# Attention with a tanh softcap, then soft mixture-of-experts slots: transposes, logits and slot sums at fixed steps of a two-quad period

## The chip, the core and the metric

The kernel runs on one core of one Trainium2 chip. Its engines work side by side, each with its own instruction queue: TensorE (PE) for matmuls and transposes into PSUM, VectorE (DVE), ScalarE (ACT), GpSimd (POOL), and SyncE (SP), which here only issues transfers. GpSimd issues transfers as well. The metric is the device time in microseconds (us) from start to end of one execution.

## What is computed

Eight batches of twelve heads, 448 positions, head size 64, float32 inputs; then a soft mixture of experts over all 3584 positions with 32 slots.

```python
scores = (q @ k.T) / sqrt(64)                 # per batch and head: 448 x 448
scores = cap * tanh(scores / cap)             # cap = 30
attn = exp(scores - max); attn /= attn.sum()  # over keys
x = concat_heads(attn @ v)                    # 3584 x 768

logits = x @ phi                              # 3584 x 32
d = exp(logits - max over positions); d /= d.sum(over positions)
slot_input = d.T @ x                          # 32 slots x 768, four slots per expert
slot_out[e] = relu(slot_input[e] @ w1[e]) @ w2[e]        # 8 experts, 768 -> 1024 -> 768
c = softmax(logits over slots)
out = c @ slot_out                            # 3584 x 768
```

The maxima are not subtracted in the kernel: tanh bounds the scores by 30, and the logits are small.

## The kernel before

**Quads, pairs, tiles, chunks.** A *quad* `Q` is four heads of one batch; three quads make a batch, 24 quads the whole. `load(Q)` fetches q, k and v of a quad with three transfers on SP (L119), each into a float32 tile of which there is one buffer, so a new load waits until the old content has been cast. `cast` (L126, VectorE) makes bfloat16 of q or k; `transp` (L134) transposes it on TensorE in seven 128x128 pieces and copies the result from PSUM (L136, VectorE) to `qT` or `kT`, two buffers each. `vcast` (L144, L145, GpSimd) puts v into one of two block-diagonal tiles `vbd` with a column of ones, which yields the row sums.

A quad is two *pairs* of heads (48 pairs). A pair has `NT` = 7 *tiles* of keys, numbered c = 0 to 6. Four tiles, wherever a pair begins or ends, make a *chunk* (`CH` = 4; 84 chunks). The chunk is the unit of ScalarE's work: one tanh (L170) over four PSUM banks of scores `sc`, one exp (L173) in place on the bfloat16 result `ex`. `sc` has one buffer of four banks: the scores of chunk j+1 (`qk_chunk`, L164, eight matmuls) can start only when the tanh of chunk j has read it, so they are made while ScalarE does the exp of chunk j.

`pv_tile` (L185) multiplies one tile of `ex` with `vbd`: four matmuls into two PSUM banks, `pv0` and `pv1`, one buffer each. A pair accumulates over its seven tiles. After the last (c = 6) VectorE takes the reciprocal of the row sums and scales, once for each bank (L194, L195), into `xq`. The next pair's first matmul into a bank waits until that bank has been read.

**Behind a pair.** `x_transp` (L207, L209) transposes the pair's part of `xq` with four transposes and a copy. `logits` (L217, L222) multiplies a quad's two transposed pairs with phi in eight matmuls and adds to the batch's sum. After a batch's third quad `e_exp` (L225) takes the exponential on ScalarE, and `slot_sums` (L237) accumulates d.T @ x and the sum of d in 28 matmuls, in three parts, with an addition to the running sum (L244) at the end. All these PSUM results, and those of `transp`, share one pool `psT` of two banks; a slot sum holds one of the two from its first part to its last.

**The order.** The order of each engine's instructions is written out by hand: the program issues each engine's instructions in the order of the Python calls, and waits between engines follow from the data. Small jobs are put by `at(j, ...)` into a list of chunk j. The main loop (L293) issues for each chunk j:

```python
tanh_chunk(j)
pv_tile of the four tiles of chunk j-1
the jobs of list j
qk_chunk(j + 1)
exp_chunk(j)
```

Before, a job's chunk follows from its own quad or pair: casts four chunks ahead of the quad's first, and so on (L257 to L276). The transfers of the expert weights w1 and w2 (32 of them, L280) are spread over the chunks on GpSimd's queue; the remaining eight blocks of w2 (L317) follow when the memory of the attention stage becomes free.

**The tail.** After the last chunk the remaining jobs run, then the expert matmuls (L337, L388), the combine weights (`ET4`, L367) and the output (L401 to L408).

Of the kernel before, what the change touches and what calls it, by code (L numbers as in the profile page):

```python
# [16 lines left out]
NT = 7  # L17
DH = 64
S = 448
CH = 4  # L20
# [7 lines left out]
def kernel(  # L28
# [22 lines left out]
    NQB = H // 4  # L51
    NQ = B * NQB
    NPAIR = 2 * NQ
    NTILE = NPAIR * NT
    NCH = NTILE // CH
# [99 lines left out]
    def qk_chunk(j):  # L155
        sc = psS.tile([P, CH, 512], F32, name="sc", tag="sc")
        scores[j] = sc
        for u in range(CH):
            pr, c = divmod(j * CH + u, NT)
            Q, h = divmod(pr, 2)  # L160
            r = slice(h * HP, h * HP + HP)
            for i in range(2):
                cs = slice(i * HP, i * HP + HP)
                pe.matmul(sc[cs, u, 0:S], qkT["k", Q][r, c, cs],  # L164
                          qkT["q", Q][r, :, cs], start=True, stop=True)

    def tanh_chunk(j):
        ex = exps.tile([P, CH, S], BF16, name="ex", tag="ex")
        exs[j] = ex
        act.activation(ex, scores.pop(j)[:, :, 0:S], ACT.Tanh, scale=qk_scale / cap)  # L170

    def exp_chunk(j):
        act.activation(exs[j], exs[j], ACT.Exp, scale=cap)  # L173

    def pv_tile(t):
        j, u = divmod(t, CH)
        pr, c = divmod(t, NT)
        Q, h = divmod(pr, 2)
        if c == 0:
            pvs[pr] = [psV.tile([P, 2, VW], F32, name=f"pv{s}", tag=f"pv{s}")  # L180
                       for s in range(2)]
            if h == 0:
                xq[Q] = xs.tile([P, NG, 2 * P], BF16, name="xq", tag="xq")
        for g in range(NG):
            pe.matmul(pvs[pr][g // 2][:, g % 2, :],  # L185
                      exs[j][:, u, GOFF[g]:GOFF[g] + P],
                      vbds[Q % 2][:, h, c, :],
                      start=(c == 0 and g % 2 == 0), stop=(c == NT - 1),
                      skip_group_check=True)
        if c == NT - 1:  # L190
            for s in range(2):
                pv = pvs[pr][s].rearrange("p g (i w) -> p g i w", i=2)
                rec = xs.tile([P, 2, 2, 1], F32, name="rec", tag="rec", bufs=4)
                dve.reciprocal(rec, pv[:, :, :, DH:DH + 1])  # L194
                dve.tensor_tensor(  # L195
                    xq[Q][:, 2 * s:2 * s + 2, h * P:(h + 1) * P]
                    .rearrange("p g (i d) -> p g i d", i=2),
                    pv[:, :, :, 0:DH],
                    rec.to_broadcast([P, 2, 2, DH]), op=ALU.mult)
            pvs.pop(pr)  # L200
# [48 lines left out]
    aux = {}  # L249

    def at(j, f, *a):
        aux.setdefault(max(j, 0), []).append((f, a))

    def first_chunk(Q):
        return Q * 2 * NT // CH

    for Q in range(1, NQ):  # L257
        j0 = first_chunk(Q)
        at(j0 - 4, cast, "k", Q)
        at(j0 - 4, cast, "q", Q)  # L260
        at(j0 - 3, transp, "k", Q)
        at(j0 - 3, vcast, Q)
        if Q + 1 < NQ:
            at(j0 - 3, load, Q + 1)
        at(j0 - 2, transp, "q", Q)
    for pr in range(NPAIR):
        jc = (pr * NT + NT - 1) // CH + 1
        Q, h = divmod(pr, 2)
        b, hq = divmod(Q, NQB)
        at(jc + 1, x_transp, pr)  # L270
        if h == 1:
            at(jc + 2, logits, Q)
            if hq == NQB - 1:
                at(jc + 3, e_exp, b)
                for part in range(3):
                    at(jc + 4 + part, slot_sums, b, part, 3)  # L276
    nw = len(wjobs)
    for n, job in enumerate(wjobs):
        j = 2 + n * (NCH - 8) // nw
# [12 lines left out]
    qk_chunk(0)  # L292
    for j in range(NCH):  # L293
        tanh_chunk(j)
        if j > 0:
            for t in range((j - 1) * CH, j * CH):
                pv_tile(t)
        for f, a in aux.pop(j, []):
            f(*a)
        if j + 1 < NCH:  # L300
            qk_chunk(j + 1)
        exp_chunk(j)
    for t in range((NCH - 1) * CH, NCH * CH):
        pv_tile(t)
# [10 lines left out]
    for n0 in range(R2, len(blocks), 4):  # L315
        t = tl.tile([P, 4, D], BF16, name=f"w2t{n0}")
# [129 lines left out]
```

The softmax here doesn't subtract the row's maximum and nothing guards it: scores larger than these inputs give would overflow.

## Time and profile before

| | us |
|---|---|
| median of three runs | 377.85 (368.37, 377.85, 377.98) |
| profiled execution, its own time | 366.62 |
| its span, first to last instruction | 364.5 |
| first tanh starts | 10.88 |
| last exp ends, about | 299.7 |

Busy time in three stretches of the profiled execution, from the profile's table of stretches (us; in brackets the number of instructions):

| stretch | PE | DVE | ACT | POOL | granted PE clock | DMA engines busy |
|---|---|---|---|---|---|---|
| 0 to 10.88 | 3.56 (22) | 3.92 (4) | 1.28 (1) | 8.63 (20) | 1.00 | 0.79 |
| 10.88 to 299.70 | 211.35 (2878) | 130.72 (356) | 277.19 (175) | 66.46 (80) | 0.98 | 0.74 |
| 299.70 to 364.50 | 41.51 (416) | 23.91 (43) | 16.62 (22) | 4.46 (6) | 0.69 | 0.85 |

The middle stretch is the attention stage, 289 of 364.5 us. The granted clock is a share of TensorE's full speed; it comes from the records of the trace. Transfers that are issued there take, from issue to landing, in the median: q 3.5 us, k 4.3, v 3.6 (448 KB each), w1 6.6 (512 KB), w2 8.2 (768 KB).

A profile names for each idle stretch of an engine what ended it (the releaser). The "chain of work that ended last" goes back from the last instruction of the execution, at each step to what released it, or to the instruction ahead of it on its engine.

### The profile page before, as it was taken

Reading aid. Unit: us, or ns where it says so; the run is one execution under the profiler, and the core shown is the slowest. Engines: PE = TensorE matmul, PEld = TensorE weight load, DVE = VectorE, ACT = ScalarE, POOL = GpSimd, SP = SyncE. Lnnn points to the kernel's source line nnn. Section 1 sums busy time; section 2 is a strip of 40 time slices with the busy share of each in tenths; the row PEclk is TensorE's granted clock in tenths of the full one; section 3 lists DMA queues with packets and bytes.
Section 4 is the critical chain, followed back from the end, with each engine's and each line's share of the span. In section 5 each row is a group of like instructions: output and inputs, shape, how many; then the busy total and the mean of one; then the engine's idle time right before and its main releaser. Section 6 shows DMA issues by size and latency. Waiting matters only on the chain.

```text
span 364.5 us, 7663 instructions
## 1 busy us (share of the span) xinstructions
PE 256.4 (70%) x3316; PEld 171.0 (47%) x3316; DVE 158.5 (43%) x403; ACT 295.1 (81%) x198; POOL 79.5 (22%) x106
## 2 busy tenths in 40 slices
PE   2868787767687767686867777778667666687581
PEld 1546455545455545464645545555545443354120
DVE  4244535435444454444553545445435324224452
ACT  1798979999999999999999999999999980214341
POOL 8321231023113230232032302321223004000000
PEclk9998969999999999999999999999999995969755
DMA  8768749476858668667696697899994808993997
GB/s 217 241 160 173 202 140 225 115 199 179 201 114 227 172 177 192 187 187 183 156 217 176 155 245 173 206 228 218 202 237 65 151 2 137 210 175 122 396 398 294
DMA packets 39409, 69.75 MB, mean 191 GB/s; under 512 B 3024, under 2 KB 29648, under 8 KB 39376
## 3 DMA queue, kind: packets, MB, share of 16 engines
q0 software_dynamic: 15760, 25.22, 38.6%
q1 hardware_dynamic: 23616, 44.05, 36.8%
q8 instruction: 26, 0.43, 0.4%
q14 instruction: 7, 0.06, 0.0%
HBM read 83.46 MB, written 11.01 MB: 259 GB/s over the span
## 4 chain that ended last, share of the span: by engine, by line
ACT 51%; PE 23%; DVE 11%; DMA 9%; issue 2%; SPq 0%; DVEq 0%; POOL 0%
ACT ex L173 26%; ACT ex L170 25%; PE pv L185 9%; PE sc L164 7%; DVE xq L195 5%; DMA w2t<-in_moe_w_dram 5%; DMA out_dram<-ob 3%; DVE ob L405 2%; PE so_ps L388 2%; DVE rec L194 2%; PE kps L134 2%; DMA kraw<-in_k_dram 1%; PE op L401 1%; PE qps L134 1%; DVE qT L136 1%
## 5 line engine op out<-in xcount | busy, mean ns | idle before, releaser
L185 PE MATMUL pv<-vbd,ex 128*128 128x130 bf16 x1344 | 107.0, 225 | 69.0 <-ACT ex L173 36.5
L170 ACT ACTIVATE ex<-sc 128x1792 bf16<-128x1792 f32 x84 | 138.9, 1654 | 18.0 <-PE sc L164 17.9
L173 ACT ACTIVATE ex<-ex 128x1792 bf16<-128x1792 bf16 x84 | 142.5, 1696 | 2.4
L185 PEld LDWEIGHTS <-ex 128*128 128x128 bf16 x1344 | 79.8, 100 | 116.1 <-ACT ex L173 71.2
L164 PE MATMUL sc<-qT,kT 64*64 64x448 bf16 x672 | 73.3, 369 | 4.6 <-ACT ex L170 1.9
L144 POOL CAST vbd<-vraw 64x896 bf16<-64x896 f32 x24 | 22.3, 928 | 203.2 <-PE pv L185 199.6
L194 DVE RECIPROCAL rec<-pv 128x4 f32<-128x4 f32 x96 | 17.1, 178 | 71.7 <-PE pv L185 71.7
L195 DVE TENSOR_TENSOR xq<-pv,rec 128x256 bf16<-128x256 f32 x96 | 40.8, 425 | 3.3
L164 PEld LDWEIGHTS <-kT 64*64 64x64 bf16 x672 | 29.1, 107 | 20.3 <-issue 3.3
L136 DVE COPY qT<-qps 128x896 bf16<-128x896 bf16 x24 | 15.0, 624 | 45.0 <-PE qps L134 45.0
L209 DVE COPY xT<-xps 128x512 bf16<-128x512 bf16 x48 | 20.1, 418 | 14.2 <-PE xps L207 14.2
L407 ACT ACTIVATE ob<-op,winv 128x768 f32<-128x768 f32 x14 | 12.5, 901 | 13.6 <-DMA out_dram<-ob 7.2
L401 PE MATMUL op<-so,ET 128*128 128x384 bf16 x56 | 18.1, 425 | 7.6 <-DVE ob L405 4.8
L145 POOL CAST vbd<-vraw 64x896 bf16<-64x896 f32 x24 | 23.0, 957 | 1.4
L207 PE MATMUL xps<-ident,xq 128*128 128x128 bf16 x192 | 19.3, 223 | 3.9 <-DVE qT L136 3.7
L136 DVE COPY kT<-kps 128x896 bf16<-128x896 bf16 x24 | 14.9, 620 | 12.7 <-PE kps L134 12.7
L405 DVE TENSOR_SCALAR ob<-op,winv 128x768 f32<-128x768 f32 x14 | 14.1, 1017 | 11.6 <-DMA out_dram<-ob 6.4
L134 PE MATMUL qps<-ident,qbf 128*128 128x128 bf16 x168 | 14.2, 228 | 5.1 <-DVE qbf L126 5.1
L126 DVE CAST kbf<-kraw 128x896 bf16<-128x896 f32 x24 | 16.0, 667 | 2.7 <-DMA kraw<-in_k_dram 2.7
L280 POOL DMA_DIRECT2D w1b<-in_moe_w_dram x24 | 17.0, 709 | 0.0
L126 DVE CAST qbf<-qraw 128x896 bf16<-128x896 f32 x24 | 15.2, 634 | 4.0 <-DMA qraw<-in_q_dram 4.0
L134 PE MATMUL kps<-ident,kbf 128*128 128x128 bf16 x168 | 14.5, 231 | 2.5 <-DVE kbf L126 2.5
(56 smaller groups left out, 152.4 us busy)
## 6 DMA issues: line engine op xcount, KB each, us to landing
w1b<-in_moe_w_dram POOLq DMA_DIRECT2D x24, 512.0 KB, 6.6
qraw<-in_q_dram SPq DMA_DIRECT2D x24, 448.0 KB, 3.5
kraw<-in_k_dram SPq DMA_DIRECT2D x24, 448.0 KB, 4.3
vraw<-in_v_dram SPq DMA_DIRECT2D x24, 448.0 KB, 3.6
out_dram<-ob SPq DMA_DIRECT2D x28, 384.0 KB, 4.5
w2b<-in_moe_w_dram POOLq DMA_DIRECT2D x8, 768.0 KB, 8.2
w2t<-in_moe_w_dram POOLq DMA_DIRECT2D x8, 768.0 KB, 12.1
phib<-in_moe_phi_dram POOLq DMA_DIRECT2D x1, 48.0 KB, 5.5
```

The source lines that it names most:

```text
L126: dve.tensor_copy(t.rearrange("p c (h d) -> p h c d", h=2), raws.pop((nm, Q)).rearrange("p h (c d) -> p h c d", d=DH))
L134: pe.transpose(ps[:, c, :], src[:, c, :], ident)
L136: dve.tensor_copy(t, ps)
L144: pool.tensor_copy(t[0:HP, :, :, 0:DH], raw[0:HP])
L145: pool.tensor_copy(t[HP:P, :, :, DH + 1:VW - 1], raw[HP:P])
L164: pe.matmul(sc[cs, u, 0:S], qkT["k", Q][r, c, cs], qkT["q", Q][r, :, cs], start=True, stop=True)
L170: act.activation(ex, scores.pop(j)[:, :, 0:S], ACT.Tanh, scale=qk_scale / cap)
L173: act.activation(exs[j], exs[j], ACT.Exp, scale=cap)
L185: pe.matmul(pvs[pr][g // 2][:, g % 2, :], exs[j][:, u, GOFF[g]:GOFF[g] + P], vbds[Q % 2][:, h, c, :], start=(c == 0 and g % 2 == 0), stop= ...
L194: dve.reciprocal(rec, pv[:, :, :, DH:DH + 1])
L195: dve.tensor_tensor(xq[Q][:, 2 * s:2 * s + 2, h * P:(h + 1) * P] .rearrange("p g (i d) -> p g i d", i=2), pv[:, :, :, 0:DH], rec.to_broadc ...
L401: pe.matmul(op[:, half, 0:HD], ET4[:, bb, c, :, :].rearrange("p a q -> p (a q)"), so[:, half, :], start=True, stop=True)
```

## The change

The lists of jobs are filled by a period of `PER` = 7 chunks, which are 28 tiles, four pairs, two quads. With m the number of the period and "step" the chunk number mod 7, a job stands at:

| step | tiles whose PV is issued in it | before, between PV and scores | after |
|---|---|---|---|
| 0 | c = 3 4 5 6 | kT transposes of an odd quad, vcast, x transpose | logits, kT transposes, vcast, q cast |
| 1 | 0 1 2 3 | qT transposes, x transpose (and a slot part) | qT transposes, x transpose |
| 2 | 4 5 6, 0 | logits (and a slot part) | x transpose (and a slot part) |
| 3 | 1 2 3 4 | k and q casts, x transpose (and a slot part) | logits, x transpose, k cast (and a slot part) |
| 4 | 5 6, 0 1 | kT transposes of an even quad, vcast (and a slot part) | kT transposes, vcast, q cast |
| 5 | 2 3 4 5 | qT transposes, x transpose (and a slot part) | qT transposes (and a slot part) |
| 6 | 6, 0 1 2 | k and q casts, logits (and a slot part) | x transpose, k cast (and a slot part) |

A comma in the second column is the turn from one pair to the next inside a chunk. Slot sums come once per batch, every ten or eleven chunks, now in two parts instead of three. The x transpose of a pair comes one chunk later for three of every four pairs; logits and `e_exp` follow one chunk later; each q cast stands one chunk behind its k cast. The weight transfers keep their chunks.

The main loop changes as well. In a chunk with a turn (steps 2, 4, 6), all jobs are issued after the old pair's last matmuls and ahead of the new pair's first. In a chunk without one, the first half of the jobs (rounded up) goes between PV and scores, as before, and the rest behind the scores. At the end, the last pairs' jobs are drawn forward where possible: chunk 83 gets x transposes of pairs 45 and 46 and the logits of quad 22.

```diff
-    for Q in range(1, NQ):
-        j0 = first_chunk(Q)
-        at(j0 - 4, cast, "k", Q)
-        at(j0 - 4, cast, "q", Q)
-        at(j0 - 3, transp, "k", Q)
-        at(j0 - 3, vcast, Q)
-        if Q + 1 < NQ:
-            at(j0 - 3, load, Q + 1)
-        at(j0 - 2, transp, "q", Q)
-    for pr in range(NPAIR):
-        jc = (pr * NT + NT - 1) // CH + 1
-        Q, h = divmod(pr, 2)
+    PER = 2 * 2 * NT // CH
+
+    def quad_in(Q, jk, jq):
+        if 0 < Q < NQ:
+            at(jk - 1, cast, "k", Q)
+            at(jk, transp, "k", Q)
+            at(jk, vcast, Q)
+            at(jq - 1, cast, "q", Q)
+            at(jq, transp, "q", Q)
+            if Q + 1 < NQ:
+                at(jq, load, Q + 1)
+
+    def pair_out(pr, j):
+        if 0 <= pr < NPAIR:
+            at(j, x_transp, pr)
+
+    def quad_out(Q, j):
+        if not 0 <= Q < NQ:
+            return
+        at(j, logits, Q)
         b, hq = divmod(Q, NQB)
-        at(jc + 1, x_transp, pr)
-        if h == 1:
-            at(jc + 2, logits, Q)
-            if hq == NQB - 1:
-                at(jc + 3, e_exp, b)
-                for part in range(3):
-                    at(jc + 4 + part, slot_sums, b, part, 3)
+        if hq == NQB - 1:
+            at(j + 1, e_exp, b)
+            at(j + 2, slot_sums, b, 0, 2)
+            at(j + 3, slot_sums, b, 1, 2)
+
+    for m in range(NCH // PER + 1):
+        j0 = m * PER
+        late = m == NCH // PER
+        quad_in(2 * m + 1, j0, j0 + 1)
+        pair_out(4 * m - 2, j0 - 1 if late else j0 + 1)
+        pair_out(4 * m - 1, j0 + 2)
+        quad_out(2 * m - 1, j0 + 3)
+        pair_out(4 * m, j0 + 3)
+        quad_in(2 * m + 2, j0 + 4, j0 + 5)
+        pair_out(4 * m + 1, j0 + 6)
+        quad_out(2 * m, j0 + 6 if m == NCH // PER - 1 else j0 + 7)
...
         tanh_chunk(j)
-        if j > 0:
-            for t in range((j - 1) * CH, j * CH):
-                pv_tile(t)
-        for f, a in aux.pop(j, []):
+        ready = list(range((j - 1) * CH, j * CH)) if j else []
+        turn = next((n for n, t in enumerate(ready) if n and t % NT == 0), len(ready))
+        for t in ready[:turn]:
+            pv_tile(t)
+        jobs = aux.pop(j, [])
+        first = len(jobs) if turn < len(ready) else (len(jobs) + 1) // 2
+        for f, a in jobs[:first]:
             f(*a)
+        for t in ready[turn:]:
+            pv_tile(t)
         if j + 1 < NCH:
             qk_chunk(j + 1)
+        for f, a in jobs[first:]:
+            f(*a)
         exp_chunk(j)
```

More of the change, by code (lines that the diff above doesn't have):

```diff
@@ L252, in at @@
         aux.setdefault(max(j, 0), []).append((f, a))
-    def first_chunk(Q):
-        return Q * 2 * NT // CH
-    for Q in range(1, NQ):
-        j0 = first_chunk(Q)
-        at(j0 - 4, cast, "k", Q)
-        at(j0 - 4, cast, "q", Q)
-        at(j0 - 3, transp, "k", Q)
-        at(j0 - 3, vcast, Q)
-        if Q + 1 < NQ:
-            at(j0 - 3, load, Q + 1)
-        at(j0 - 2, transp, "q", Q)
-    for pr in range(NPAIR):
-        jc = (pr * NT + NT - 1) // CH + 1
-        Q, h = divmod(pr, 2)
-        b, hq = divmod(Q, NQB)
-        at(jc + 1, x_transp, pr)
-        if h == 1:
-            at(jc + 2, logits, Q)
-            if hq == NQB - 1:
-                at(jc + 3, e_exp, b)
-                for part in range(3):
-                    at(jc + 4 + part, slot_sums, b, part, 3)
+    PER = 2 * 2 * NT // CH
[15 more added lines that the diff above has]
+        at(j, logits, Q)
+        b, hq = divmod(Q, NQB)
+        if hq == NQB - 1:
[13 more added lines that the diff above has]
+        quad_out(2 * m, j0 + 6 if m == NCH // PER - 1 else j0 + 7)
     nw = len(wjobs)
```

## The prediction

> **What bounds the kernel now.** I read the page's list of the costliest groups first, then the waits, then ScalarE's row of the timeline, then the chain of work that ended last. The groups (columns: line, engine, operation, output and input, count | busy us, mean ns of one | idle time before them, and what ended it):
>
> ```profile
> L185 PE MATMUL pv<-vbd,ex 128*128 128x130 bf16 x1344 | 107.0, 225 | 69.0 <-ACT ex L173 36.5
> L170 ACT ACTIVATE ex<-sc 128x1792 bf16<-128x1792 f32 x84 | 138.9, 1654 | 18.0 <-PE sc L164 17.9
> L173 ACT ACTIVATE ex<-ex 128x1792 bf16<-128x1792 bf16 x84 | 142.5, 1696 | 2.4
> ```
>
> ScalarE works 281 us on 84 tanh and 84 exp, and waits 17.9 us for scores. Of these, 8.9 us are the wait for the first chunk. So the attention stage is bound by ScalarE, and all that a change of TensorE's order can win is the time by which scores come late. The first tanh starts at 10.88, the last at 296.32: 285.44 us for 83 chunks. A chunk that waits for nothing takes 3.28 us from tanh to tanh (289.76, 293.04, 296.32 in the timeline), so 83 x 3.28 = 272.2 and the **excess is 13.2 us**.
>
> I call chunk number mod 7 its step: 7 chunks are 4 pairs, so the pattern repeats. Differences of tanh starts, summed by step over the 12 periods, give the excess as: step 0 0.4, step 1 1.9, step 2 0.6, step 3 0.2, **step 4 5.8**, step 5 0.6, **step 6 3.7**. Steps 4 and 6 are those in which the last matmuls of one pair and the first of the next stand in one chunk with few of the old pair ahead. In undisturbed periods step 4 takes 3.59 and step 6 3.57, with slot sums 3.79 both. The chain shows why (start, us, what):
>
> ```profile
> 153.25 0.30 PE pv L185 x2
> 153.56 0.02 issue
> 153.58 0.20 DVE rec L194
> 153.77 0.02 issue
> 153.79 0.42 DVE xq L195
> 154.22 0.10 DVE rec L194
> 154.32 0.02 issue
> 154.34 0.44 DVE xq L195
> 154.78 0.05 issue
> 154.83 0.74 PE pv L185 x10
> 155.57 0.19 PE lps L217 x8
> 155.76 0.89 PE sc L164 x8
> ```
>
> The reader sees a step 6: TensorE ends the pair, stands idle while VectorE empties both PSUM banks (1.2 us), then does the next pair's matmuls, then eight matmuls of logits, and only then the scores. The idle stretch and the logits lie one behind the other. The waits say the same in sum:
>
> ```profile
> PE pv L185 <- DVE xq L195: 23.5, 60, 0.6
> ACT ex L170 <- PE sc L164: 17.9, 28, 8.9
> ```
>
> [...]there is a half-clock spell (mean clock 0.84 in 35 to 57 us; 16 PV matmuls took 1.92 us there at 45.74, 1.08 elsewhere). [...]at 137.64 a weight load of L207 runs 0.70 us before its matmul, which waits. [...]here both pv tiles have one buffer, and the 23.5 us above are the price.
>
> **The change, part by part.** No matmul, copy, activation or transfer is added or removed; all are moved.
>
> *Key transposes in step 4.* Seven transposes (0.48 us from the first, 148.52, to the scores, 149.00) went between PV and scores. Now they stand after the old pair's 8 matmuls, ahead of the new pair's, in the 1.2 us in which TensorE waits for VectorE. Step 4 was 3.59; the chain without them gives 3.11, under 3.28, so excess 0. Nine plain or slot periods win 0.31 or 0.50 each, slot matmuls leaving this step too (0.20). The two in the cold clock: chunk 4 (4.17) loses 0.55 and keeps 0.34; chunk 11 (4.83; scores at 52.63, last PV behind them at 51.64) loses 0.99 and keeps 0.56. Step 4: 5.8 to 0.9.
>
> *Step 6.* Logits (0.28 from 155.41 to 155.69 by the timeline) go to step 0, where no pair turns. In their place one x transpose of 4 (0.27 by weight loads) and, every second period, 16 slot matmuls (8 take 0.31, so 0.62) stand in the idle stretch: from 153.48 (PV weights end) to 154.28, 0.80 us. 0.27 is hidden; 0.89 overhangs by 0.09, but the second bank is free only at 154.83, which leaves room. Scores then start at 155.41, tanh 0.99 later at 156.40: 3.30 against 3.28. I keep 0.05 each, as the price of a tanh that still just waits. Step 6: 3.7 to 0.55. If cover fails, the 0.27 to 0.89 come back one to one.
>
> *Step 1.* Six chunks lose 0.36: a third tile wanted one of two transpose banks while the slot sums held the other, so x transposes waited for the copy of qT (0.52 idle at 137.66 to 138.34 before L207). Now slot sums are not in step 1, and its x transpose goes behind the scores. There it delays only the next PV: scores from 1.67 to 2.61 after tanh, four transposes to 2.9, next PV not before 3.42. The start-up chunk (0.45, transposes at half clock) stays. Step 1: 1.9 to 0.45.
>
> *Steps 0, 2, 3, 5.* Logits, x transposes and slot sums move into steps with room: PV 0.9, slot 0.62, logits 0.28 end 1.95 after tanh, scores may start at 2.37. The 0.5 of chunk 9 falls to about 0.1 (half clock). The small exponential (L225) stays on ScalarE, 0.05 in each of 7 places. These four: 1.8 to 0.8.
>
> *Casts and loads.* POOL's and SP's orders are unchanged. Each q cast goes one step later, behind the evacuation and the kT copy on VectorE, and frees the raw buffer for the next q load; k is queued behind q on SP. In step 4 that cast now ends 3.2 us after tanh (148.11 end of xq, kT copy 0.62, cast 0.62, less 146.22), so k is issued at 149.8 of the old clock instead of 144.15, and beside v and a weight load of POOL. The next k cast is due in step 6, 5.1 us later. k lands in 4.3 us in the median, 6.5 at most. VectorE may stand there until 157.4 before the transposes make scores late (step 0 at 156.06; scores by +2.47, less 0.48 for transposes and 0.62 for the cast). That is **7.6 us from issue to landing**. I cost it at 0. A k cast moved alone costs nothing: its data came long before.
>
> *Tail.* Chunk 83 gains two x transposes and logits, ends PV 3.36 after tanh, and the last PV start at 3.43: 0. The old x transpose after the last PV stood in VectorE's shadow: 0. The 64.8 us behind the last exp are untouched.
>
> **Sum.** Left of 13.2: 0.9 + 0.55 + 0.45 + 0.8 = 2.7, so the gain is 10.5 us. Profiled execution: 366.62 (span 364.5 and 2.1 around it) to 356.1. The runs shown are 368.37, 377.85 and 377.98. The profiled one stands 11.2 below their median and 1.75 below the lowest, which I take as the same mode: 368.37 - 10.5 = **358**. From the median it would be 367.3; the trace cannot show what the 10 us between the runs are, so this is the range's upper part.
>
> **Rivals.** *Half of it stays.* The turns still end late: VectorE, with xT and casts queued behind the evacuation, or TensorE's own pace lets tanh wait 0.15 in all 23 turns of steps 4 and 6 (3.5 us), and the cold spells cost what they did (1.9). Gain 5.1: 361.5 profiled, 363.3 against the lowest run: within 2%. For it: step 6 comes out at 3.30 with no room. Against: step 4 has 0.17.
>
> *Keys come late.* The q, k and v loads now queue together with a 512 or 768 KB weight load. [...]If k takes more than 7.6 us, VectorE stands at the cast with the next reciprocal behind it, and TensorE at the transposes: at 10 us, 2.4 us in each of 11 periods, 26 less 10.5 = 16 slower, 382 to 384. It decides from 8.6 us on, where it eats the gain. Against it: 6.5 is the longest k seen, and v beside a weight load takes 3.6.
>
> *It does not do what it says*, since a transpose in the gap could wait for the evacuation it should cover. By the code x transposes in a gap read a pair that ended two or more chunks before; only chunk 83 reads the fresh one. Then about 366 to 368.
>
> **How the numbers follow.** Forecast 0.72, half stays 0.16, late keys 0.08, no effect 0.04. A change of 2% (7.3 us) is about what a measurement of this kernel can tell from none. Faster by more: 0.72; within, with the half and no effect: 0.20; slower: 0.08. The gain lies between 5 and 13.2: 353 to 363 from the two lower bases, and up to 368 if the timed runs are of the kind of the median. Range 353 to 368.
>
> **What would show it.** Steps 4 and 6 at 3.28 to 3.35; tanh's wait for scores 10 to 11 us, 8.9 of them the first; waits of PV for xq well under 23.5; span about 354; ScalarE's share of the chain from 51% to 70% or more. Wrong: a wait of the k cast for its DMA beyond the start, or steps 4 and 6 still at 3.5.

## The result, and the profile after

| | before | changed |
|---|---|---|
| median of the runs shown, us | 373.11 (367.37 to 377.98, 4 runs) | 384.53 (380.92 to 387.94, 4 runs) |
| profiled execution, us | 366.62 | 384.37 |
| its span | 364.5 | 382.3 |
| attention stage, first tanh to last exp, about | 288.8 | 305.9 |
| TensorE's granted clock in that stage | 0.98 | 0.89 |

The changed kernel is slower: the ratio of its times to those before is 1.041 (95% interval 1.031 to 1.051). The prediction said 358 and is wrong; of its rivals, the one with the late keys named the mechanism and the time (382 to 384). Runs of one kernel differ by up to 7%, so each ratio leaves out those more than 1.5% above their kernel's fastest; the profiled execution of the kernel before is one of its fastest, and those of before_q_late, q_two_buffers, spread and warm_before are among their kernel's slower ones.

From the page of the kernel before, the shares of its chain of work by engine ("issue" is time in which the engine waited for nothing that the profile shows; a name with q is the engine's instruction queue), its group of k casts (columns as in the prediction) and its k transfers (number, size, median us from issue to landing):

```profile
ACT 51%; PE 23%; DVE 11%; DMA 9%; issue 2%; SPq 0%; DVEq 0%; POOL 0%
...
L126 DVE CAST kbf<-kraw 128x896 bf16<-128x896 f32 x24 | 16.0, 667 | 2.7 <-DMA kraw<-in_k_dram 2.7
...
kraw<-in_k_dram SPq DMA_DIRECT2D x24, 448.0 KB, 4.3
```

The same of the changed kernel, with some groups more:

```profile
DMA 35%; PE 20%; ACT 20%; DVE 13%; issue 7%; SPq 2%; POOL 1%; DVEq 0%; ACTq 0%; POOLq 0%
...
L170 ACT ACTIVATE ex<-sc 128x1792 bf16<-128x1792 f32 x84 | 138.9, 1653 | 35.4 <-PE sc L164 35.2
...
L126 DVE CAST kbf<-kraw 128x896 bf16<-128x896 f32 x24 | 15.3, 639 | 42.0 <-DMA kraw<-in_k_dram 42.0
...
L134 PE MATMUL kps<-ident,kbf 128*128 128x128 bf16 x168 | 15.8, 244 | 17.7 <-DVE kbf L126 17.6
...
kraw<-in_k_dram SPq DMA_DIRECT2D x24, 448.0 KB, 7.3
vraw<-in_v_dram SPq DMA_DIRECT2D x24, 448.0 KB, 8.6
```

ScalarE's own work is what it was, 138.9 us of tanh. Its wait for scores has doubled, 17.9 to 35.2. The new name in the list is the k cast: VectorE stands 42.0 us in front of it, waiting for the k transfer, where it stood 2.7 before. The median k transfer now lands 7.3 us after its issue, not 4.3. A chain of which transfers hold 35%, 9% before, in a stage that ScalarE bounds, says that something arrives late.

The timeline shows one case (start, duration, engine, line, operation; in brackets the idle time before it and what ended it; lines that do not bear on it are left out). It is the k of an even quad, whose cast stands at the end of step 3 and whose transposes stand in step 4:

```profile
117.82 1.41 POOL L294 DMA_DIRECT2D w1b<-in_moe_w_dram  x2
118.39 0.37 SPq L119 DMA_DIRECT2D qraw<-in_q_dram  x1
118.81 0.46 SPq L119 DMA_DIRECT2D kraw<-in_k_dram  x1
119.36 0.43 SPq L119 DMA_DIRECT2D vraw<-in_v_dram  x1
...
126.71 0.63 PE L185 MATMUL pv<-vbd,ex 128*128 128x130 bf16 x8 [0.79 <-ACT ex L173]
...
128.30 0.63 DVE L126 CAST kbf<-kraw 128x896 bf16<-128x896 f32 x1 [2.89 <-DMA kraw<-in_k_dram]
128.84 0.18 DVE L194 RECIPROCAL rec<-pv 128x4 f32<-128x4 f32 x1
128.98 0.56 PE L134 MATMUL kps<-ident,kbf 128*128 128x128 bf16 x7 [1.64 <-DVE kbf L126]
129.62 1.29 PE L185 MATMUL pv<-vbd,ex 128*128 128x130 bf16 x8
130.84 1.33 PE L164 MATMUL sc<-qT,kT 64*64 64x448 bf16 x8
132.11 1.92 PE L185 MATMUL pv<-vbd,ex 128*128 128x130 bf16 x16
132.21 1.66 ACT L170 ACTIVATE ex<-sc 128x1792 bf16<-128x1792 f32 x1 [2.27 <-PE sc L164]
```

Two weight transfers are issued, and within 1.6 us all three loads of the next quad. k lands 9.5 us after its issue, at 128.3. The pair's PV is done at 127.3, but its reciprocal (128.84) is queued on VectorE behind the k cast, and TensorE's transposes wait for the same cast. ScalarE gets its scores 2.27 us late. After that comes a second effect: the scores and the sixteen PV matmuls behind them take 1.33 and 1.92 us, against 0.76 and 1.08 elsewhere. The table of stretches shows the reason (columns: length of the stretch; busy us, with the number of instructions, of PE, PE's weight loads, DVE, ACT and POOL; granted clock; busy share of the transfer engines; GB/s):

```profile
124.00:128.00 4.00, 2.52 (x38) 1.73 (x34) 0.66 (x2) 3.97 (x3) 0.00 (x0) 1.00 1.08 291
128.00:132.00 4.00, 2.86 (x23) 1.45 (x23) 2.72 (x7) 1.91 (x2) 2.36 (x3) 0.71 0.20 74
132.00:136.00 4.00, 4.00 (x33) 2.93 (x31) 0.62 (x1) 3.36 (x2) 0.56 (x1) 0.50 0.91 211
136.00:140.00 4.00, 3.76 (x30) 2.31 (x28) 1.45 (x5) 3.36 (x2) 0.00 (x0) 0.50 0.82 247
```

TensorE stood idle (in the 3.41 us from 126.24 to the fall it is busy for 1.22), its clock fell to half, and in steps 5 and 6, which wait for no key, it alone held ScalarE up (5.65, 4.23 and 4.51 us for steps 4, 5 and 6, where 3.28 is free of waits). The clock records of these traces know only full and half (1.00 and 0.50), so a mean clock gives the time at half: 68 us of the attention stage (mean 0.888), 10 before (0.982). All amounts of half clock below are such sums over that stage; the expectations, which counted whole stretches of 1 us, have some of them 1 or 2 us higher.

The excess over 83 x 3.28 us, summed from the differences of tanh starts as in the prediction (profiled executions):

| step | 0 | 1 | 2 | 3 | 4 | 5 | 6 | sum |
|---|---|---|---|---|---|---|---|---|
| before | 0.4 | 1.9 | 0.6 | 0.2 | 5.8 | 0.6 | 3.7 | 13.2 |
| changed | 6.9 | 2.1 | 0.8 | 0.2 | 11.5 | 4.5 | 4.4 | 30.3 |
| changed, q cast put back | 0.3 | 1.7 | 0.6 | 0.6 | 0.7 | 0.0 | 2.6 | 6.5 |
| the same, with idle matmuls | 0.2 | 1.0 | 0.1 | 0.4 | 0.2 | 0.0 | 1.1 | 3.0 |

Steps 0 and 4, where late keys strike, hold 18.4 of the 30.3; steps 1, 5 and 6, which follow them, 11.0, where they held 6.2 before. The last two rows are experiments of the next section.

### The profile page after: what moved, and what is told of

Read it like the earlier page. It is cut to its first block, busy times and chain, and to the rows that moved or that the text cites. A ratio compares the mean times of both kernels' runs of the same rounds, so it can differ in the third digit from the quotient of the medians.

```text
span 382.3 us, 7663 instructions
## 1 busy us (share of the span) xinstructions
PE 283.9 (74%) x3316; PEld 184.2 (48%) x3316; DVE 161.6 (42%) x403; ACT 294.9 (77%) x198; POOL 82.5 (22%) x106
## 4 chain that ended last, share of the span: by engine, by line
DMA 35%; PE 20%; ACT 20%; DVE 13%; issue 7%; SPq 2%; POOL 1%; DVEq 0%; ACTq 0%; POOLq 0%
DMA kraw<-in_k_dram 27%; ACT ex L173 10%; ACT ex L170 10%; PE pv L185 8%; PE sc L164 7%; DMA w2t<-in_moe_w_dram 5%; DVE xq L195 4%; DMA out_dram<-ob 3%; DVE qbf L126 2%; DVE kbf L126 2%; PE so_ps L409 2%; PE qps L134 1%; DVE kT L136 1%; DVE rec L194 1%; SPq L429 1%
## 5 line engine op out<-in xcount | busy, mean ns | idle before, releaser
L170 ACT ACTIVATE ex<-sc 128x1792 bf16<-128x1792 f32 x84 | 138.9, 1653 | 35.4 <-PE sc L164 35.2
L185 PE MATMUL pv<-vbd,ex 128*128 128x130 bf16 x1344 | 117.2, 239 | 46.4 <-ACT ex L173 29.2
L185 PEld LDWEIGHTS <-ex 128*128 128x128 bf16 x1344 | 88.2, 106 | 94.3 <-ACT ex L173 57.5
L164 PE MATMUL sc<-qT,kT 64*64 64x448 bf16 x672 | 82.4, 403 | 3.4 <-ACT ex L170 1.6
L144 POOL CAST vbd<-vraw 64x896 bf16<-64x896 f32 x24 | 23.1, 962 | 218.0 <-DMA vraw<-in_v_dram 111.7
L164 PEld LDWEIGHTS <-kT 64*64 64x64 bf16 x672 | 31.1, 115 | 25.0 <-issue 10.8
L134 PE MATMUL kps<-ident,kbf 128*128 128x128 bf16 x168 | 15.8, 244 | 17.7 <-DVE kbf L126 17.6
L145 POOL CAST vbd<-vraw 64x896 bf16<-64x896 f32 x24 | 24.8, 1035 | 1.4
L428 ACT ACTIVATE ob<-op,winv 128x768 f32<-128x768 f32 x14 | 12.5, 900 | 13.3 <-DMA out_dram<-ob 8.7
L126 DVE CAST qbf<-qraw 128x896 bf16<-128x896 f32 x24 | 20.8, 866 | 3.9 <-DMA qraw<-in_q_dram 3.9
L134 PEld LDWEIGHTS <-kbf 128*128 128x128 bf16 x168 | 11.5, 109 | 20.4 <-DVE kbf L126 20.3
L134 PE MATMUL qps<-ident,qbf 128*128 128x128 bf16 x168 | 16.8, 254 | 5.5 <-DVE qbf L126 5.5
## 6 DMA issues: line engine op xcount, KB each, us to landing
w2b<-in_moe_w_dram POOLq DMA_DIRECT2D x8, 768.0 KB, 10.2
```

What stands on the lines that cost most here:

```text
L126: dve.tensor_copy(t.rearrange("p c (h d) -> p h c d", h=2), raws.pop((nm, Q)).rearrange("p h (c d) -> p h c d", d=DH))
L134: pe.transpose(ps[:, c, :], src[:, c, :], ident)
L144: pool.tensor_copy(t[0:HP, :, :, 0:DH], raw[0:HP])
L145: pool.tensor_copy(t[HP:P, :, :, DH + 1:VW - 1], raw[HP:P])
L164: pe.matmul(sc[cs, u, 0:S], qkT["k", Q][r, c, cs], qkT["q", Q][r, :, cs], start=True, stop=True)
L185: pe.matmul(pvs[pr][g // 2][:, g % 2, :], exs[j][:, u, GOFF[g]:GOFF[g] + P], vbds[Q % 2][:, h, c, :], start=(c == 0 and g % 2 == 0), stop= ...
```

## The experiments

The theory: each q cast one step later holds the one float32 q buffer longer; the q load, and k behind it on SP, go out together with the weight transfers; k lands late; VectorE and TensorE stand in line behind its cast. Rivals: the new places of the transposes starve TensorE into half clock by themselves; or the late v is what hurts.

**q_cast_back**: one line of the lists undone.

```diff
             at(jk - 1, cast, "k", Q)
+            at(jk - 1, cast, "q", Q)
...
-            at(jq - 1, cast, "q", Q)
```

> The changed kernel with each q cast put back beside its k cast, one step earlier, as before; all else as changed. Late keys: the q and k loads go out 3 to 4 us earlier, ahead of the weight loads, k lands in 4 to 5 us again (7.3 in the changed kernel), VectorE's wait at the k cast falls from 42 us to under 5, excess of the attention stage over 83 x 3.28 us falls from 30.3 to 2 to 5, profiled time 354 to 359, ratio to before about 0.97. Rival (the new places of transposes and sums put TensorE to half clock by themselves): tanh still waits over 25 us for scores, 375 or more.

361.53 us (359.83 to 365.12), ratio 0.982 (0.969 to 0.995). The waits of this kernel that answer to those above (us in total, number of times, longest):

```profile
ACT ex L170 <- PE sc L164: 12.5, 7, 8.8
...
DVE kbf L126 <- DMA kraw<-in_k_dram: 3.3, 2, 2.6
```

One cast put back turns 4% slower into some 2% faster. k lands in 4.3 us, VectorE waits 3.3 us at the k cast, 2.6 of them at the start. The excess is 6.5, a little above what was expected: 2.2 of it lies in chunks 1 to 3, at the start, and some 1.5 in half-clock spells that begin in step 6.

**before_q_late**: the opposite, that one edit in the kernel before.

```diff
-        at(j0 - 4, cast, "q", Q)
...
         at(j0 - 3, vcast, Q)
+        at(j0 - 3, cast, "q", Q)
```

> The kernel before with one edit: each q cast one step later, behind the k transposes and the v cast. Late keys: k lands in 7 us or more, VectorE waits 30 to 45 us at the k cast, excess 13.2 grows to 35 or more, 385 to 397 us. Rival (the new places do it): no change, 366 to 370.

393.41 us, ratio 1.064 (1.052 to 1.076). k lands in 7.5 us, and VectorE waits 65.7 us at the k cast, more than expected:

```profile
DVE kbf L126 <- DMA kraw<-in_k_dram: 65.7, 20, 5.7
```

The edit alone costs 6%, so the loss of the changed kernel needs nothing else of the change. With q_cast_back this clears the new places of the transposes as its main cause.

**k_first**: the q cast stays late, and only the order of the loads is changed.

```diff
-        for nm, src in (("q", q), ("k", k), ("v", v)):
+        order = (("q", q), ("k", k), ("v", v)) if Q == 0 else (("k", k), ("q", q), ("v", v))
+        for nm, src in order:
```

> The changed kernel, q casts still late, but each quad's loads are issued in the order k, q, v in place of q, k, v (quad 0 as before). The k load then waits only for the k cast and goes out one step earlier. If what hurts is that k stands behind q on SP's queue: k lands in 4 to 5 us, VectorE's wait at the k cast under 5 us, excess 2 to 5, 354 to 360 us; q lands late (6 us or more) but is due three steps later. If the late v and the weight loads behind v's cast are what hurts, or any load in that place: 370 or more.

364.02 us, ratio 0.987 (0.979 to 0.995). k lands in 4.0 us, q in 6.3, v in 8.2. Its waits:

```profile
POOL vbd L145 <- DMA vraw<-in_v_dram: 81.1, 9, 10.3
ACT ex L171 <- PE sc L165: 12.5, 7, 8.8
DVE kbf L127 <- DMA kraw<-in_k_dram: 3.0, 2, 2.1
```

v is almost as late as in the changed kernel (8.2 us against 8.6), GpSimd waits 81.1 us for it, and ScalarE does not feel it: scores wait 12.5 us, as with the q cast put back. That rules out the late v as the cause of the loss. What hurt was k's place behind q on SP.

**q_two_buffers**: the late cast and the load order kept, a second buffer for the float32 q.

```diff
-            t = ld.tile([P, 2, S], F32, name=nm + "raw", tag=nm + "raw")
+            t = ld.tile([P, 2, S], F32, name=nm + "raw", tag=nm + "raw",
+                        bufs=2 if nm == "q" else 1)
```

> The changed kernel, its late q casts and its load order q, k, v kept, but with two buffers for the float32 q in place of one. The q load then waits for the q cast of a quad before, and k behind it on SP goes out with its own cast, one step earlier. If the late q cast hurts only through the one buffer and SP's order: VectorE waits under 5 us at the k cast, excess of the attention stage 5 to 8, 359 to 365 us. If VectorE's order with the late q cast is itself harmful: 370 or more.

364.63 us (357.45 to 367.12), ratio 0.975 (0.970 to 0.981), from the three lowest of 17 runs; the two medians alone give 0.984. VectorE waits 3.1 us at the k cast:

```profile
DVE kbf L127 <- DMA kraw<-in_k_dram: 3.1, 2, 2.5
```

The late q cast hurts only through the one buffer. The profiled execution, 365.95, has 34 us of half clock, most of it in spells of 6.8 us that begin in step 6 and take up to 1.4 us there and 0.6 to 0.8 in the next step 0; its excess is 12.2, not 5 to 8.

**weights_last**: the changed kernel with its 32 weight transfers behind the attention stage.

```diff
-        j = 2 + n * (NCH - 8) // nw
+        j = NCH + 8
```

> The changed kernel with its 32 weight transfers issued after the attention stage; the time as a whole grows by the transfers at the end (some 80 us) and is not compared; read the attention stage alone, up to the last exp. If the weight loads beside the k load make it late: k lands in 4 to 5.5 us although it is issued as late as in the changed kernel, excess 2 to 6. If the late issue alone is enough: VectorE still waits over 20 us at the k cast, excess over 15.

437.49 us in a single run, which counts the transfers moved to the end; only the attention stage is read. k, issued as late as in the changed kernel, lands in 4.4 us (6.4 at most), and VectorE waits 5.7 us at its cast in all:

```profile
DVE kbf L126 <- DMA kraw<-in_k_dram: 5.7, 4, 3.0
```

So it takes both: late issue and the weight transfers beside it. The changed kernel's own trace shows how k depends on them. Where two weight transfers were issued in the 1.0 us ahead of k, k took 9.3 to 11.1 us (eight loads); where one was, 6.8 to 7.7 (three loads); where none was and the next came 1.3 us or more later, 4.4 to 5.0 (six loads). The other five, with one 0.3 us behind k, took 5.0 to 9.7.

The excess, 12.8, missed the 2 to 6 that I expected. It comes from 37 us of half clock that no late key explains. Stretches of this run at the onset of one such spell, all before any wait for a key (columns as above):

```profile
52.40:53.20 0.80, 0.63 (x8) 0.15 (x3) 0.28 (x1) 0.80 (x1) 0.00 (x0) 1.00 0.98 372
53.20:54.00 0.80, 0.18 (x4) 0.19 (x5) 0.00 (x0) 0.80 (x2) 0.00 (x0) 1.00 1.05 401
54.00:54.80 0.80, 0.44 (x8) 0.27 (x5) 0.62 (x3) 0.80 (x1) 0.00 (x0) 1.00 1.07 408
54.80:55.60 0.80, 0.50 (x6) 0.33 (x7) 0.77 (x4) 0.77 (x2) 0.00 (x0) 1.00 0.94 358
55.60:56.40 0.80, 0.80 (x12) 0.54 (x11) 0.60 (x2) 0.80 (x1) 0.00 (x0) 0.80 0.06 20
56.40:57.20 0.80, 0.80 (x8) 0.36 (x4) 0.00 (x0) 0.65 (x1) 0.00 (x0) 0.50 0.00 0
```

Between the scores of step 5 and the end of step 6's gap TensorE is busy 1.12 of 2.4 us; then the clock halves. This raised a second question, which the last runs ask.

**loop_only** and **lists_only** take the change apart: the changed main loop with the lists of before, and the changed lists (q cast put back) with the main loop of before. The edit of loop_only, in the kernel before; lists_only has it the other way round:

```diff
         tanh_chunk(j)
-        if j > 0:
-            for t in range((j - 1) * CH, j * CH):
-                pv_tile(t)
-        for f, a in aux.pop(j, []):
+        ready = list(range((j - 1) * CH, j * CH)) if j else []
+        turn = next((n for n, t in enumerate(ready) if n and t % NT == 0), len(ready))
...
+        for f, a in jobs[first:]:
+            f(*a)
         exp_chunk(j)
```

> The kernel before, with its own lists of jobs, and only the changed main loop: jobs between the pairs in a chunk with a turn, half of them behind the scores otherwise. If the placement in the gap brings the gain: steps 4 and 6 fall from 3.57 to 3.79 to 3.28 to 3.40, excess from 13.2 to 5 to 8, 359 to 364 us, k lands in 4.3 us. If the new lists are needed for it: 366 or more.

363.47 us, ratio 0.984 (0.972 to 0.995). Step 4 falls to 3.28, step 6 to 3.38 outside half-clock spells, but 44 us of half clock bring the excess of the profiled execution to 13.7, against the 5 to 8 expected.

> The changed lists with the q cast put back, but the main loop of before (all jobs between PV and scores). If the placement brings the gain: steps 4 and 6 stay at 3.5 to 3.6 (the transposes and x transposes stand on the way to the scores), only step 1's slot cases are won, excess 9 to 12, 363 to 367 us. If the lists bring it: excess under 8, 358 to 363.

369.41 us, ratio 0.995 (0.990 to 1.001): no gain that can be told from none. The excess of its profiled execution is 11.6. Step 4 takes 3.58 to 3.60 in eleven periods of twelve, step 6 3.60 or more. The median is above what I expected, 363 to 367. The gain comes from the place in the gap; the new lists add nothing that was measured, and they brought in the late q cast.

**spread**: with the q cast put back, the first pair's x transpose moved to step 5.

```diff
-        pair_out(4 * m, j0 + 3)
+        pair_out(4 * m, j0 + 5)
```

> The changed kernel with the q cast put back, and the first pair's x transpose moved from step 3 to step 5, where only the q transposes stand. If half-clock spells that begin in step 6 come from TensorE being sparse in steps 5 and 6: fewer of them than 2 to 4 in a run, excess 4 to 5, 1 to 3 us faster than with the q cast put back alone. If they come by chance: no difference, 359 to 365 us.

367.06 us, ratio 0.987 (0.967 to 1.007), 44 us of half clock in the profiled execution. Not fewer spells, and not faster. But the run says little about sparseness: the transpose went ahead of the scores of step 5, not behind them, and the idle time behind them only fell from 0.79 us to 0.71 (at 125.5 with the q cast put back, at 126.3 here).

**warm_q_cast_back** and **warm_q_two_buffers**: matmuls that nobody reads, put into the idle time behind the scores of step 5.

```diff
+    warm = consts.tile([P, 512], BF16, name="warm")
+    pool.memset(warm, 1.0)
...
             qk_chunk(j + 1)
+        if j % 7 == 5:
+            wm = psT.tile([P, 512], F32, name="wm", tag="T")
+            for n in range(3):
+                pe.matmul(wm, ident, warm, start=True, stop=True)
```

> The changed kernel with the q cast put back, and three idle matmuls of 512 columns (identity times ones, result read by nobody) on TensorE behind the scores of each step 5, in the 0.8 us that TensorE stands idle there. If half-clock spells begin because TensorE is sparse between the scores of step 5 and the first PV of step 6: spells in the attention stage fall from 16 us to under 6, excess from 6.5 to about 4 (the start-up's 2 to 3 stay), 358 to 360 us. If they come by chance: no difference, 359 to 365.

356.36 us (355.55 to 361.57), ratio 0.966 (0.955 to 0.977). Half clock falls from 15 us to none, the excess from 6.5 to 3.0. Some 1.2 us of the gain are not the clock's: the first tanh starts at 9.64, not 10.88, with a first k cast of 0.65 us, not 1.74. The wait for scores, of which the first chunk is 7.6 here:

```profile
ACT ex L172 <- PE sc L166: 8.3, 2, 7.6
```

> The same three idle matmuls in the changed kernel with two q buffers, where the profiled run had 34 us of half clock and an excess of 12.2. If sparse TensorE is the cause: under 10 us of half clock, excess 4 to 6, 357 to 360 us, 4 us or more faster than without. If not: 363 to 367.

355.06 us (352.74 to 356.70), ratio 0.962 (0.954 to 0.970): the fastest of all. Against the runs of the kernel before beside each, its median stands at 0.964 and that of q_two_buffers at 0.984. 3 us of half clock remain of 34.

The same three matmuls as controls, in the changed kernel and in the one before:

> The changed kernel, late q casts and all, with the three idle matmuls in step 5. They can prevent spells that begin in step 6, not those that begin while TensorE waits for late keys. If late keys are the main cost: VectorE still waits 35 us or more at the k cast, 60 us or more of half clock, 378 to 386 us. If the spells of step 6 are: under 370.

379.47 us (375.01 to 384.14) against 369.28 before. VectorE waits 34.3 us at the k cast, 41 us of half clock stay, a little less of both than expected. The late keys, not the spells of step 6, are the main cost of the change.

> The kernel before with the same three idle matmuls in step 5. Its turns still end late in steps 4 and 6 (0.30 each), and its profiled run had only 12 us of half clock: excess 10 to 12, 362 to 368 us, ratio 0.985 to 1.0. If half clock rather than the turns made up its excess: under 360.

380.53 us, ratio 1.020 (1.009 to 1.032): a miss. The lowest of four runs, 374.27, is above all seven of the kernel before beside them. The profiled execution has 61 us of half clock, 11 of its 13 spells beginning in step 4. It is the longest of the four runs (386.35), and the 10 us before are from one of the shortest, so the difference of 51 us is not the matmuls' alone. Still, idle matmuls are no cure by rule. The last section shows which places they fill and which they leave; whether they harm this kernel by themselves is open.

## Why the prediction was wrong

1. *The bound*: right. Where nothing is late, a chunk takes 3.28 us in every kernel tried, and the time follows the scores.

2. *Step 4*: 5.8 was to fall to 0.9. With the q cast put back it is 0.7, and 0.2 without half clock. The key transposes are hidden behind the evacuation, as the sum had it.

3. *Step 6*: 3.7 was to fall to 0.55. It is 1.1 (3.38 eleven times) without half clock and 2.6 with it. With the gap filled the scores start 0.67 us after the second bank's first PV, not 0.58 as I took from the start of the logits; each such step keeps 0.10, twice the 0.05 that I allowed. The half-clock spells were not in the sum.

4. *Step 1 and the small steps*: 0.45 and 0.8 were to be left; the kernel with idle matmuls has 1.0 and 0.7, the start-up costing more than I took. The sum of 2.7 compares with 3.0 measured there.

5. *Casts and loads, "I cost it at 0"*: **the step that failed.** The limit of 7.6 us was about right: a k load that landed after 6.9 us cost step 0 nothing, and one issued at the same place that took 7.7 cost it 0.65. The landing time was not: I took 4.3 (6.5 at most) from a kernel in which q and k go out alone, ahead of the weight transfers, and moved the issue into a place where they go out with v and one or two weight transfers. There it is 7.3 in the median, up to 11.1. And I priced only the odd quads' k, issued in step 4; the even quads' k, issued behind the q cast of step 0 and so at the start of step 1, was never worked out, and step 4, where it is due, holds the largest loss, 11.5. A wait of the k cast beyond the start was the first of the signs that I had named for being wrong.

6. *Half clock*: I had read its spells in the trace (mean clock 0.84 in 35 to 57 us) and gave it no price beyond those that the kernel before had (chunks 4 and 11). The steps that follow a late key (1, 5, 6) cost 11.0 us, where the sum left 1.0 for steps 1 and 6 and at most 0.8 for step 5.

7. *The rival "keys come late"*: right in its place and, by chance in part, in its size. It priced 2.4 us in eleven periods; in fact both quads of a period can be late, some are not, and half clock adds to it. Its chance of 0.08 was too small: in 200 to 250 us of the trace of before the transfer engines are 88% busy, and every load that I moved was moved into the busiest place of its queue, which called for a landing time from such a place. The trace of before had no load of q or k in such a place; v, which goes out there alone, took 3.6 in the median and 7.9 once, and I read the 3.6.

8. *Tail*: right. From the last exp to the end 64.8 us before, 65.4 after.

"Half of it stays" does not describe the changed kernel. It fits the repaired ones at 0.975 to 0.987, but for the half clock and not for the reason I gave.

## What to carry to other kernels

A cast that frees a single load buffer is the issue time of the next load: when it moves, find what else that moment releases (here weight transfers, all set free by the same turn of a pair), and take the landing time from a place as crowded. VectorE, held at the k cast by a late transfer, ran the reciprocal queued behind it 1.5 us late (at 128.84), so here the load needed first should stand first in its queue; the order k, q, v cost one line and brought k in after 4.0 us, not 7.3. And the gain of filling an evacuation gap on TensorE was real and, with the idle matmuls, as large as worked out (the excess fell by 10.2 us, against 10.5), but a part of it came only when the clock was kept up: 3.5 us of excess with the q cast put back, 7.0 with two buffers.

## What the runs showed of the hardware that I had not expected

Half clock also began without any long wait of TensorE: in weights_last it is busy for 1.12 of 2.4 us before the fall shown above, and in the 3.41 us ahead of that fall no idle piece is longer than 0.79 us.

In the traces of the kernel before and of the changed one, the spells that begin in the attention stage last 3.41 to 13.65 us. In the 3.41 us (as long as the shortest spell) ahead of each of these eleven falls TensorE is busy for 1.17 to 2.15 us, a share of 0.34 to 0.63; over the whole stage its share is 0.73 before and 0.78 in the changed kernel. (Busy is what the matmul records show; of the idle matmuls of warm_after and warm_before only 24 of 36 are recorded.)

A sparse place in TensorE's order was not always followed by half clock. In the kernel before, the most sparse 3.41 us of a regular period have a busy share of 0.53 to 0.54 (in steps 0 to 2), 0.47 to 0.51 (3 to 4) and 0.48 to 0.57 (5 to 6), and still its clock stays full from 54.5 us to the last tanh, 242 us on. Which of such places are followed by half clock, no run has shown.

The idle matmuls stand in step 5 alone. With the q cast put back they raise the lowest share of 3.4 us around step 6 of a regular period from 0.56 to 0.77 (worked out from the tables by 1 us), and half clock falls from 15 us to none. In warm_before, the eleven spells of step 4 follow stretches of 3.4 us with a share of 0.50 to 0.60, by the same tables. This was read from the traces afterwards; no run set the busy share to test it.
